# Gates worked out slot by slot, and key and value loads asked for one pair of chunks earlier

## The chip, the cores and the metric

The kernel runs on one core of a Trainium2 chip. The metric is device time in microseconds (us) from start to end of one execution, as a median of several. A profiled execution gives the trace from which every row below comes; its span runs from the first to the last recorded instruction. PE is the matrix engine, DVE the vector engine, ACT the scalar engine, POOL the general engine (it also issues the indirect DMAs, by row numbers in a table), SP the queue that issues the plain DMAs. DMA engines are the sixteen engines that move the data.

## The reference

Two stages. The first is an attention with 32 memory slots for each of 8 heads and 8 batches of 576 tokens; the second a mixture of experts that sends each token to one of 8 experts.

```python
a = softmax(phi, over the 576 tokens)
k_m, v_m = a^T k, a^T v                       # 32 x 64 for each batch and head
attn = softmax(q k_m^T / 8)                   # 576 x 32
x = (attn v_m), heads side by side            # 4608 rows of 512
logits = x @ w_gate                           # 8 for each row
e = argmax(logits)
gate = softmax(logits)[e]
eom = sigmoid((x @ w_output_gate)[e])
out = gate * eom * (relu(x @ w1[e]) @ w2[e])  # 512 -> 1024 -> 512
```

So each row of x needs its 8 gate logits, 8 logits of the output gate, the number of its expert, and one factor, gate * eom, that is multiplied into its output row. All is in fp32; the expert products are made with a high and a low part of each operand.

## The kernel before, in words

**The head: attention.** The batches go in four pairs. Of each pair, `memory` builds the memory keys and values from nine chunks of k and v: `turn_a` transposes the softmaxed phi (tile `ph`) into `at`, `sums` multiplies it with the chunk of k and v (tile `kvt`, or `kv8` for the ninth) into `pk`. `loads` is a generator that asks for k and v, two chunks at each step; `sums` steps it once for each pair of chunks that it uses, so `NLD`, the number of steps taken ahead, is how many pairs of chunks are asked for before their use. `kvt` has 8 buffers. Queries (`qt`, three buffers) are asked for by `load_q` right behind the `scores` that used the buffer. The twenty groups of rows (five to a pair) each go through `scores` (PE), `shift` (DVE transposes and takes the maximum, POOL subtracts), `expo` (ACT), `divide` (DVE sum and reciprocal, POOL multiplies), `back` (DVE transposes) and `values` (PE, then ACT copies to `xo`). The list `ORDER` is walked once for each group and sets the order of these pieces of different groups on each engine.

**Rows in DRAM.** `store` writes the finished rows to `xs`. A row has 576 numbers: four parts of 144, each with 128 numbers of x and 16 partial logits (8 of the gate, 8 of the output gate), since the logits ride along in `values`. The fifth group of a pair holds the last 64 tokens of both its batches and is stored by two transfers of 64 rows (L1058). SP works strictly in order, so a store that waits for its rows holds back every load behind it. `defer` puts a function off by a count of steps of `ORDER`; its counts stand in `LATE`.

**Ranking.** When a pair is done, `rank` sums the partial logits (`lg`), finds each row's expert and its place within the expert (DVE, a few small products on PE), and works out gate * eom. `gates_out` then writes this factor, 16 times side by side, over the first 16 partial logits of each row in `xs`: 64 bytes a row, four transfers for a pair. The one-hot rows `Aw` (POOL) and `table` make the lists of rows by which POOL gathers.

**The body: slots.** A slot is up to three blocks of 128 rows of one expert. Here 14 run: five whole slots of three blocks while attention still goes on, then five of three blocks and four of two whose rows are gathered by quarters of a row (`quart`). For each, POOL gathers `xg`, `turn_x` transposes it into a high and a low part, and `several` makes the two products, eight units of weights `w` per slot. ACT casts each to its high part (L587), DVE subtracts for the low part (L602), both into a ring `whl`. After every twelve products of the first half, and after each unit and block of the second, `hook` takes some steps of the pieces that are left: attention, ranking, gathers, stores put off (`kept`, `singly`). `finish_y` multiplies each output row by its factor and scatters it. The body opens at the 18th group (`START`).

Of the kernel before, what the change touches and what calls it, by code (L numbers as in the profile page):

```python
# [48 lines left out]
NLD = 2  # L49
# [8 lines left out]
LATE = {"lg": 8, "w": 2, "ct": 8, "pe": 3, "dve": 2}  # L58
# [13 lines left out]
def attention_moe(tc, phiT, kv, qT, wgo, wall, out):  # L72
# [3 lines left out]
    with contextlib.ExitStack() as ctx:  # L76
# [615 lines left out]
        def loads():  # L692

            load_phi(0)
            for bp in range(NBP):
                for c in (0, 2, 4, 6):
                    load_kv(bp, c)
                    load_kv(bp, c + 1)
                    if bp == 0 and c == 2:
                        load_kv(0, 8)  # L700
                        load_q(0)
                        load_q(1)
                    if bp == 0 and c == PHI1:
                        load_phi(1)
                    if bp == 0 and c == 6:
                        for n in range(2, NQ):
                            load_q(n)
                    if bp == NBP - 1 and c == 6:
                        stream.fetch()
                    yield  # L710

# [220 lines left out]
        def rank(bp, lg):  # L932

            t0 = bp * 2 * S
            lt = lg[:, :, 0:E]
            lo = lg[:, :, E:2 * E]
# [4 lines left out]
            w2_ = rt.tile(b3, F32, name="w2_")  # L941
            w3_ = rt.tile(b3, F32, name="w3_")
            pm = rt.tile([P, NCH], F32, name="pm")
            zs = rt.tile([P, NCH], F32, name="zs")
            gd = rt.tile([P, NCH], F32, name="gd")
# [4 lines left out]
            gt = rt.tile([P, NCH, XQ - P], F32, name="gt")  # L950
# [6 lines left out]
            G.tensor_tensor(w2_[:], lt, lmb, ALU.subtract)  # L957
# [8 lines left out]
            V.tensor_tensor(w3_[:], oh, lo, ALU.mult)  # L966
            A.activation(w2_[:], w2_[:], AF.Exp)
# [5 lines left out]
            V.tensor_reduce(zs[:], w3_[:], axis=AX.X, op=ALU.add)  # L973
            yield

            def rest():
# [10 lines left out]
                V.tensor_reduce(gd[:], w2_[:], axis=AX.X, op=ALU.add)  # L987
                A.activation(zs[:], zs[:], AF.Exp, scale=-1.0)
# [4 lines left out]
                V.tensor_scalar(gd[:], gd[:], 1e-9, None, ALU.add)  # L993
# [3 lines left out]
                V.tensor_scalar(zs[:], zs[:], 1.0, None, ALU.add)  # L997
# [3 lines left out]
                V.tensor_tensor(gd[:], gd[:], zs[:], ALU.mult)  # L1001
                yield
                V.tensor_copy(row[:], ri[:])  # L1003
                V.reciprocal(gd[:], gd[:])
                yield
                V.tensor_copy(gt[:], gd[:].unsqueeze(2).to_broadcast([P, NCH, XQ - P]))
                def gates_out(b):
                    nc.sync.dma_start(
                        xs[t0 + b * S:t0 + b * S + 512, P:XQ].rearrange("(c p) d -> p c d", p=P),
                        gt[:, 4 * b:4 * b + 4])  # L1010
                    nc.sync.dma_start(xs[t0 + b * S + 512:t0 + b * S + 576, P:XQ], gt[64 * b:64 * b + 64, 8])
# [4 lines left out]
                if bp == 1 and "open" not in env:  # L1016
                    kept.extend(functools.partial(gates_out, b) for b in range(2))
                    singly.extend(functools.partial(one_hot, c) for c in range(NCH))
                else:
                    for b in range(2):  # L1020
                        gates_out(b)
                    for c in range(NCH):
                        one_hot(c)
                        if c % 3 == 2:
                            yield
# [17 lines left out]
        def store(bp, c2, xo, lg):  # L1043
            t0 = bp * 2 * S
            b, n = c2 // 2, 2 if c2 < 4 else 1
            if c2 < 4:
                r, w = t0 + b * S + (c2 % 2) * 256, 256 // len(xo)
                for k, t in enumerate(xo):
                    out_ = functools.partial(
                        nc.sync.dma_start, xs[r + w * k:r + w * k + w].rearrange("(c p) d -> p c d", p=P),  # L1050
                        t.rearrange("p c r d -> p c (r d)"))
                    if 5 * bp + c2 in KEPT:
                        kept.append(out_)
                    else:
                        out_()
            else:
                for b_ in range(2):
                    nc.sync.dma_start(  # L1058
                        xs[t0 + b_ * S + 512:t0 + b_ * S + 576],
                        xo[0][64 * b_:64 * b_ + 64, 0].rearrange("p r d -> p (r d)"))  # L1060
# [37 lines left out]
        def turn_x(z, c):  # L1098
# [4 lines left out]
            if c == 0:  # L1103
                z["x"] = (mo.tile([P, 4, 3 * P], F32R, name="xh"),
                          None if nb == 2 else mo.tile([P, 4, 3 * P], F32R, name="xl"))
                if z["quart"]:
                    z["xt"] = {}
                    z["g"] = env["xt"].tile([P, 3], F32, name="gx")
                    for b in range(4):
                        k = nb - (nb == 2 and b > 1)  # L1110
                        A.copy(z["g"][32 * b:32 * b + 32, 0:k], xg[0:32, 0:k, XQ * b + P])
# [25 lines left out]
            V.tensor_tensor(xl[:, c, 0:n], pt, xh[:, c, 0:n].bitcast(F32), ALU.subtract)  # L1137

# [126 lines left out]
        def finish_y(z, k, py):  # L1265
# [9 lines left out]
            A.activation(y[0:n], py[0:n], AF.Copy, scale=z["g"][0:n, k:k + 1] if z["quart"] else z["xg"][:, k, P:P + 1])  # L1275
# [4 lines left out]
        def several(i, st, nxt, hook):  # L1280


            z = order[i]
            nb, x, h = z["nb"], z["x"], []
            n_ = nb * P
            for u in range(4):
# [36 lines left out]
                hook()  # L1323
            py = [bank([DM], "ps") for _ in range(nb)]
# [26 lines left out]
        def single(i, st, nxt):  # L1351
# [15 lines left out]
            for u in range(4):  # L1367
# [13 lines left out]
                if u < 3:  # L1381
                    st.done(PUMP[1])
            for c in range(5):
                nxt(c)
# [132 lines left out]
```

## Time and profile before

| | |
|---|---|
| median of the runs shown | 546.48 us |
| lowest of them | 546.12 us |
| the profiled execution | 548.27 us |
| its span | 546.5 us |
| PE busy in the span | 508.1 us, 93% |
| DVE, ACT, POOL busy | 65%, 53%, 44% |
| mean granted clock of PE | 0.974 of 2.4 GHz |
| bytes moved by DMA | 123.54 MB, 42,062 packets |
| packets under 512 bytes | 10,320 |

Busy shares are of the whole span. A share says nothing on what a stage waits for; that is read from the timeline of an engine and from the waits.

### The profile page before, as it was taken

To read this page: it belongs to the slowest core of one execution; us is meant where nothing else is said; L and a number is where in the kernel's file an instruction comes from. 1 tells how busy PE (TensorE), PEld (TensorE's weight loads), DVE (VectorE), ACT (ScalarE), POOL (GpSimd) and SP (SyncE) were. 2 spreads that over 40 slices of the span, in tenths; PEclk is the share of its full clock that TensorE was granted. 3 is DMA by queue.
4 is the path that set the end of the run, shared out by engine and by line. 5 is a ranking of instruction groups with operands and counts; after the bars stand their busy time and mean duration, and the time that the engine had idled before them with its cause. 6 is when DMAs were issued, how large, how long until landed. Compare 5 with 4: busy or idle time off the path is not lost. (4 is left out here: it accounts for less than half of the span.)

```text
span 546.5 us, 10564 instructions
## 1 busy us (share of the span) xinstructions
PE 508.1 (93%) x3850; PEld 438.2 (80%) x3850; DVE 353.6 (65%) x783; ACT 288.1 (53%) x536; POOL 239.5 (44%) x254
## 2 busy tenths in 40 slices
PE   3888788799999999999999999999999999999993
PEld 2555465598788898898998989998999799898982
DVE  4376979978965569888455547953875397639310
ACT  3467466754445466363443547853874476458210
POOL 2244386582625045220575554465547253721101
PEclk9969879999999999999999999999999999999998
DMA  8999998998767668745566665865785577743001
GB/s 303 418 391 388 411 347 282 365 359 299 228 191 256 196 192 280 225 147 155 155 163 205 184 228 168 257 194 202 217 257 143 187 249 232 239 135 98 30 20 44
DMA packets 42062, 123.54 MB, mean 226 GB/s; under 512 B 10320, under 2 KB 10384, under 8 KB 41616
## 3 DMA queue, kind: packets, MB, share of 16 engines
q1 hardware_dynamic: 35200, 102.71, 57.2%
q0 software_dynamic: 6800, 20.06, 10.6%
q8 instruction: 32, 0.52, 0.4%
q14 instruction: 30, 0.25, 0.1%
HBM read 102.40 MB, written 20.35 MB: 225 GB/s over the span
## 5 line engine op out<-in xcount | busy, mean ns | idle before, releaser
L1340 PE MATMUL bps<-whl,hh 128*128 128x512 f32 x640 | 192.6, 393 | 0.8 <-issue 0.8
L1303 PE MATMUL bps<-xh,whl 128*128 128x384 f32 x640 | 165.8, 336 | 0.0
L602 DVE TENSOR_TENSOR whl<-w,whl 128x1024 fp32r<-128x1024 f32 x112 | 136.4, 1222 | 9.7 <-ACT whl L587 9.3
L1340 PEld LDWEIGHTS bps<-whl,hh 128*128 128x128 f32 x640 | 119.9, 188 | 25.9 <-issue 1.6
L587 ACT CAST whl<-w 128x1024 fp32r<-128x1024 f32 x112 | 116.6, 1046 | 24.8 <-remote 14.4
L1303 PEld LDWEIGHTS bps<-xh,whl 128*128 128x128 f32 x640 | 115.8, 188 | 1.2 <-issue 0.6
L542 POOL DMA_INDIRECT xg<-xs,idx_ql x84 | 99.6, 1186 | 25.6 <-issue 22.6
L1303 PE MATMUL bps<-xl,whl 128*128 128x384 f32 x320 | 107.1, 335 | 0.0
L1340 PE MATMUL bps<-whl,hl 128*128 128x512 f32 x240 | 93.6, 390 | 0.0
L1308 DVE SCALAR_TENSOR_TENSOR hl<-bps,hh 128x384 fp32r<-128x384 f32 x80 | 43.9, 554 | 66.2 <-ACT hh L1307 51.2
L1307 ACT ACTIVATE hh<-bps 128x384 fp32r<-128x384 f32 x80 | 38.9, 493 | 78.7 <-PE bps L1303 70.5
L1276 POOL DMA_INDIRECT out<-y,idx_ol x23 | 25.8, 1122 | 108.5 <-ACT y L1275 54.4
L1303 PEld LDWEIGHTS bps<-xl,whl 128*128 128x128 f32 x320 | 60.1, 188 | 0.5
L1340 PEld LDWEIGHTS bps<-whl,hl 128*128 128x128 f32 x240 | 45.1, 188 | 8.5
L885 POOL TENSOR_TENSOR ea<-ea,mx 128x512 f32<-128x512 f32 (+1 forms) x20 | 19.3, 963 | 45.8 <-DVE mx L883 38.8
L1298 PE MATMUL bps<-xh,whl 128*128 128x384 f32 x128 | 37.7, 338 | 0.0
L1299 PE MATMUL bps<-xh,whl 128*128 128x256 f32 x128 | 35.7, 279 | 0.0
L1014 POOL TENSOR_SCALAR Aw<-iota_row,row 128x128 bf16<-128x128 bf16 x36 | 29.3, 828 | 8.3 <-DVE row L1003 8.3
L1276 POOL DMA_INDIRECT out<-y,idx_ob x9 | 10.7, 1189 | 49.0 <-ACT y L1275 39.5
L1275 ACT ACTIVATE y<-bps,gx 128x512 f32<-128x512 f32 x19 | 13.1, 688 | 35.6 <-PE bps L1340 29.0
L916 PE MATMUL bpd<-ve_b,aT 64*128 64x144 f32 (+1 forms) x320 | 27.9, 325 | 2.5 <-DVE ea L879 1.4
L879 DVE STREAM_TRANSPOSE ea<-bpd 128x512 f32<-128x512 f32 (+1 forms) x20 | 13.2, 660 | 23.7 <-PE bpd L869 11.8
(277 smaller groups left out, 599.7 us busy)
## 6 DMA issues: line engine op xcount, KB each, us to landing
w<-wall SPq DMA_DIRECT2D x112, 512.0 KB
kvt<-kv SPq DMA_DIRECT2D x32, 512.0 KB
qt<-qT SPq DMA_DIRECT2D x16, 512.0 KB
xs<-xo SPq DMA_DIRECT2D x8, 576.0 KB
ph<-phiT SPq DMA_DIRECT2D x3, 1152.0 KB
kv<-kv SPq DMA_DIRECT2D x4, 512.0 KB
xg<-xs,idx_ql POOLq DMA_INDIRECT x84
ph<-phiT SPq DMA_DIRECT2D x4, 288.0 KB
```

Of the source, the lines that this page charges most:

```text
L542: G.indirect_dma_start(out=z["xg"][:, k, XQ * b:XQ * b + XQ], out_offset=None, in_=xs[0:z["rows"]].rearrange("t (a q) -> (t a) q", a=4), i ...
L587: A.copy(hl[:, 0], w[:])
L602: V.tensor_tensor(hl[:, 1], w[:], hl[:, 0].bitcast(F32), ALU.subtract)
L916: T.matmul(px[to:to + n, r, sl], z["aT"][h, o:o + n], ves[2 * bp + b][h, g], start=True, stop=True)
L1014: G.tensor_scalar(Aw[:, bp * NCH + c], iota_row[:], row[:, c:c + 1], None, ALU.is_equal)
L1276: G.indirect_dma_start(out=out, out_offset=bass.IndirectOffsetOnAxis(ap=z["idx"][1][0:n, z["q0"] + k:z["q0"] + k + 1], axis=0), in_=y[0:n] ...
L1298: T.matmul(pb, w[:, 0, o:o + P], x[0][:, cc], start=(cc == 0), stop=False)
L1299: T.matmul(pb[:, 0:256], w[:, 1, o:o + P], x[0][:, cc, 0:256], start=False, stop=(cc == 3))
L1303: T.matmul(pb, w[:, b, o:o + P], x[a][:, cc, 0:n_], start=(n == 0), stop=(n == 11))
L1307: A.activation(h_[:, j], pb, AF.Relu)
L1308: V.scalar_tensor_tensor(l_[:, j], pb, 0.0, h_[:, j].bitcast(F32), ALU.max, ALU.subtract)
L1340: T.matmul(py[k], a, w[:, b, DM * f:DM * f + DM], start=(u == 4 and f == 0 and n == 0), stop=(u == 7 and f == 1 and n == len(ps) - 1))
```

## The change

Each slot gets its rows' logits with the rows, so `gate` works the factor out there. It takes one step at every `hook` of the first half of the slot, ahead of the step of attention, and what is left is drained ahead of the second half. A whole slot sums the four partial logits in one reduction; a slot by quarters brings them together with three copies on ACT and three additions on DVE, in rows of 32 partitions, and copies the factor out by four copies (which stood in `turn_x` before). `rank` loses the matching work, and `gates_out` with its 16 transfers goes. `NLD` is 3 in place of 2, `loads` gets a step of its own at its end that asks for the first weights, and the store of the tenth group (the fifth of the second pair) is put off by five steps.

```diff
-NLD = 2
+NLD = 3
-LATE = {"lg": 8, "w": 2, "ct": 8, "pe": 3, "dve": 2}
+LATE = {"st": 5, "lg": 8, "w": 2, "ct": 8, "pe": 3, "dve": 2}
...
-                    if bp == NBP - 1 and c == 6:
-                        stream.fetch()
                     yield
+            stream.fetch()
+            yield
...
-            G.tensor_tensor(w2_[:], lt, lmb, ALU.subtract)
...
-            V.tensor_tensor(w3_[:], oh, lo, ALU.mult)
-            A.activation(w2_[:], w2_[:], AF.Exp)
...
-            V.tensor_reduce(zs[:], w3_[:], axis=AX.X, op=ALU.add)
...
-                V.tensor_reduce(gd[:], w2_[:], axis=AX.X, op=ALU.add)
-                A.activation(zs[:], zs[:], AF.Exp, scale=-1.0)
...
-                V.tensor_scalar(gd[:], gd[:], 1e-9, None, ALU.add)
...
-                V.tensor_scalar(zs[:], zs[:], 1.0, None, ALU.add)
...
-                V.tensor_tensor(gd[:], gd[:], zs[:], ALU.mult)
...
-                V.reciprocal(gd[:], gd[:])
...
-                V.tensor_copy(gt[:], gd[:].unsqueeze(2).to_broadcast([P, NCH, XQ - P]))
-                def gates_out(b):
-                    nc.sync.dma_start(
-                        xs[t0 + b * S:t0 + b * S + 512, P:XQ].rearrange("(c p) d -> p c d", p=P),
-                        gt[:, 4 * b:4 * b + 4])
-                    nc.sync.dma_start(xs[t0 + b * S + 512:t0 + b * S + 576, P:XQ], gt[64 * b:64 * b + 64, 8])
...
+                def out_():
+                    for b_ in range(2):
+                        nc.sync.dma_start(
+                            xs[t0 + b_ * S + 512:t0 + b_ * S + 576],
+                            xo[0][64 * b_:64 * b_ + 64, 0].rearrange("p r d -> p (r d)"))
+
+                if bp == 1:
+                    defer("st", out_)
+                else:
+                    out_()
...
+        def gate(z):
+
+            nb, xg, quart = z["nb"], z["xg"], z["quart"]
+            n, m = (32, 6 if nb == 2 else 4 * nb) if quart else (P, nb)
+            z["g"] = rt.tile([P, 3], F32, name="gx", bufs=2)
...
+            if quart:
...
+                for a in range(1, 4):
+                    A.copy(lq[:, a - 1, 0:m], xv[32 * a:32 * a + 32])
+                    yield
+                V.tensor_tensor(ls, xv[0:32], lq[:, 0, 0:m], ALU.add)
+                V.tensor_tensor(lq[:, 1, 0:m], lq[:, 1, 0:m], lq[:, 2, 0:m], ALU.add)
+                yield
+                V.tensor_tensor(ls, ls, lq[:, 1, 0:m], ALU.add)
+            else:
+                V.tensor_reduce(ls, xg[:, 0:nb].rearrange("p k (a q) -> p k q a", a=4)[:, :, P:XQ],
+                                axis=AX.X, op=ALU.add)
+            yield
+            V.tensor_reduce(mx, ls[:, :, 0:E], axis=AX.X, op=ALU.max)
+            V.tensor_tensor(oe[:], iota_s[:, 0:E], slot[:, z["s"]:z["s"] + 1].to_broadcast([P, E]), ALU.is_equal)
+            yield
+            V.tensor_tensor(w2, ls[:, :, 0:E], mx.unsqueeze(2).to_broadcast(b3), ALU.subtract)
+            V.tensor_tensor(w3, ls[:, :, E:2 * E], oe[0:n].unsqueeze(1).to_broadcast(b3), ALU.mult)
+            yield
+            A.activation(w2, w2, AF.Exp)
+            V.tensor_reduce(zs, w3, axis=AX.X, op=ALU.add)
+            yield
+            A.activation(zs, zs, AF.Exp, scale=-1.0)
+            V.tensor_reduce(sm, w2, axis=AX.X, op=ALU.add)
+            yield
+            V.tensor_scalar(sm, sm, 1e-9, None, ALU.add)
+            V.tensor_scalar(zs, zs, 1.0, None, ALU.add)
+            V.tensor_tensor(g, sm, zs, ALU.mult)
...
-            A.activation(y[0:n], py[0:n], AF.Copy, scale=z["g"][0:n, k:k + 1] if z["quart"] else z["xg"][:, k, P:P + 1])
+            A.activation(y[0:n], py[0:n], AF.Copy, scale=z["g"][0:n, k:k + 1])
...
+            gen = gate(z)
+
+            def hook():
+                next(gen, None)
+                hook_()
...
+            last(gen)
```

On DVE, where the first pair is ranked beside the first route (`fi`, `pt`, `ie` and `exc` belong to the route, `rki`, `ri` and `row` to the rank, `gd`, `zs` and `gt` to the gates), this stood:

```order
L991 TENSOR_TENSOR w__953<-ohg,pr 128x72
L993 TENSOR_SCALAR gd<-gd 128x9
L174 TENSOR_TENSOR pt<-fi,upto 128x64
L996 TENSOR_REDUCE rki<-w__953 128x9
L997 TENSOR_SCALAR zs<-zs 128x9
L176 TENSOR_REDUCE inc<-pt 128x8
L999 TENSOR_SCALAR ri<-rki 128x9
L1000 TENSOR_SCALAR jg<-rki 128x9
L1001 TENSOR_TENSOR gd<-gd,zs 128x9
L304 TENSOR_SCALAR ie<-inc 128x8
```

Now this stands there:

```order
L978 TENSOR_TENSOR w__957<-ohg,pr 128x72
L174 TENSOR_TENSOR pt<-fi,upto 128x64
L982 TENSOR_REDUCE rki<-w__957 128x9
L176 TENSOR_REDUCE inc<-pt 128x8
L984 TENSOR_SCALAR ri<-rki 128x9
L985 TENSOR_SCALAR jg<-rki 128x9
L304 TENSOR_SCALAR ie<-inc 128x8
```

The steps on `gd` and `zs` are gone from between the others, and nothing else changes its place.

On SP, while the second pair is worked on, this stood from the last writes of the first pair's gates (`gt`) to the last loads of k and v (`kvt`, `kv`); the two transfers of 64 rows of `xo` are the tenth group's:

```order
L1008 DMA xs<-gt 128x4x16
L1011 DMA xs<-gt 64x16
L689 DMA kvt<-kv 128x1024 x2
L684 DMA qt<-qT 128x1024
L689 DMA kv_1268<-kv 128x1024
L689 DMA kvt<-kv 128x1024 x2
L684 DMA qt<-qT 128x512
L684 DMA qt<-qT 128x1024
L1058 DMA xs<-xo 64x576 x2
L689 DMA kvt<-kv 128x1024 x2
L684 DMA qt<-qT 128x1024
L689 DMA kvt<-kv 128x1024 x2
```

Now this stands there:

```order
L689 DMA kvt<-kv 128x1024 x2
L684 DMA qt<-qT 128x1024
L689 DMA kv_1252<-kv 128x1024
L689 DMA kvt<-kv 128x1024 x2
L684 DMA qt<-qT 128x512
L684 DMA qt<-qT 128x1024
L689 DMA kvt<-kv 128x1024 x2
L684 DMA qt<-qT 128x1024
L1033 DMA xs<-xo 64x576 x2
```

The writes of `gt` are gone, the tenth group's store stands behind the last loads of k and v, and each pair of chunks is asked for one step sooner.

On DVE, in the first slot (`hl` and `whl` belong to the slot, `sa` and `aT` to attention), this stood:

```order
L1308 SCALAR_TENSOR_TENSOR hl<-bps,hh 128x384
L602 TENSOR_TENSOR whl<-w,whl 128x1024 x2
L895 TENSOR_REDUCE sa<-ea_207 128x16
L897 RECIPROCAL sa<-sa 128x16
L903 STREAM_TRANSPOSE aT<-ea_206 128x512
L1308 SCALAR_TENSOR_TENSOR hl<-bps,hh 128x384 x2
L602 TENSOR_TENSOR whl<-w,whl 128x1024
L1308 SCALAR_TENSOR_TENSOR hl<-bps,hh 128x384
```

Now this stands there (`gl`, `gs`, `oe`, `gw` and `go` are the gates' tiles):

```order
L1340 SCALAR_TENSOR_TENSOR hl<-bps,hh 128x384
L602 TENSOR_TENSOR whl<-w,whl 128x1024 x2
L1141 TENSOR_REDUCE gs<-gl 128x3
L1142 TENSOR_TENSOR oe<-iota_s,slot 128x8
L895 TENSOR_REDUCE sa<-ea_207 128x16
L897 RECIPROCAL sa<-sa 128x16
L903 STREAM_TRANSPOSE aT<-ea_206 128x512
L1340 SCALAR_TENSOR_TENSOR hl<-bps,hh 128x384
L1144 TENSOR_TENSOR gw<-gl,gs 128x24
L1145 TENSOR_TENSOR go<-gl,oe 128x24
L1340 SCALAR_TENSOR_TENSOR hl<-bps,hh 128x384
L602 TENSOR_TENSOR whl<-w,whl 128x1024
```

The gates' steps stand between those of the slot and of attention, one or two at each hook.

## Rows read from the trace of the kernel before

**Rows 1.** The page's first part: busy us (share of the span) xinstructions.

```profile
PE 508.1 (93%) x3850; PEld 438.2 (80%) x3850; DVE 353.6 (65%) x783; ACT 288.1 (53%) x536; POOL 239.5 (44%) x254
```

**Rows 2.** Timeline of PE: start, length, what, and in brackets the wait before.

```profile
62.03 0.64 PE L778 MATMUL pk<-kvt,at 128*32 128x128 f32 x16 [1.36 <-DMA kvt<-kv]
...
72.72 0.94 PE L869 MATMUL bpd<-qt,kT 64*32 64x256 f32 x16 [1.00 <-ACT kT L809]
...
75.92 2.46 PE L916 MATMUL bpd<-ve_b,aT 64*128 64x144 f32 x16
...
80.50 0.92 PE L869 MATMUL bpd<-qt,kT 64*32 64x256 f32 x16
...
111.72 0.47 PE L1303 MATMUL bps<-xh,whl 128*128 128x384 f32 x1
```

**Rows 3.** Windows: stretch, PE, PEld, DVE, ACT, POOL busy, PE clock, DMA share, GB/s.

```profile
57.00:78.50 21.50, 16.65 (x287) 11.57 (x283) 19.58 (x78) 10.19 (x25) 12.03 (x19) 0.82 1.01 377
78.50:82.40 3.90, 3.90 (x59) 2.26 (x53) 0.71 (x4) 2.47 (x6) 3.24 (x4) 0.67 0.99 381
82.40:112.00 29.60, 24.56 (x459) 16.97 (x458) 26.88 (x68) 20.56 (x43) 19.89 (x24) 0.94 0.91 320
...
111.70:125.00 13.30, 13.30 (x101) 12.17 (x100) 10.66 (x19) 6.32 (x11) 10.99 (x11) 1.00 1.01 379
125.00:150.00 25.00, 24.71 (x181) 20.41 (x181) 21.32 (x61) 12.27 (x22) 10.55 (x14) 1.00 0.81 250
```

**Rows 4.** Waits of PE from 112 us on: sum in us, times, longest.

```profile
PE bpd L916 <- DVE xl L1137: 1.1, 1, 1.1
```

**Rows 5.** Timeline of DVE in the head.

```profile
59.65 0.23 DVE L966 TENSOR_TENSOR w__955<-ohg,lg 128x72 f32<-128x72 bf16 x1
...
65.32 0.23 DVE L991 TENSOR_TENSOR w__953<-ohg,pr 128x72 f32<-128x72 bf16 x1 [0.40 <-PE pr L985]
...
66.69 0.30 DVE L1006 COPY gt<-gd 128x144 f32<-128x144 f32 x1
...
74.67 0.18 DVE L244 CAST hl_i<-pr 128x12 bf16<-128x12 f32 x1 [0.59 <-PE pr L237]
...
82.39 0.72 DVE L879 STREAM_TRANSPOSE ea<-bpd 128x512 f32<-128x512 f32 x1 [3.19 <-PE bpa L804]
...
89.41 1.33 DVE L956 TENSOR_TENSOR w__1478<-lg,lm 128x72 f32<-128x72 f32 x1
...
95.08 0.33 DVE L966 TENSOR_TENSOR w__1480<-ohg,lg 128x72 f32<-128x72 bf16 x1
...
98.60 0.62 DVE L997 TENSOR_SCALAR zs<-zs 128x9 f32<-128x9 f32 x1
...
99.72 0.30 DVE L1006 COPY gt<-gd 128x144 f32<-128x144 f32 x1
```

**Rows 6.** Windows of 3 us in the head, columns as in rows 3.

```profile
72.00:75.00 3.00, 1.89 (x34) 1.16 (x38) 2.27 (x9) 1.29 (x5) 3.00 (x7) 0.88 1.02 292
75.00:78.00 3.00, 3.00 (x46) 2.46 (x36) 2.90 (x9) 1.06 (x2) 1.21 (x2) 0.50 0.89 296
...
84.00:87.00 3.00, 2.38 (x46) 1.33 (x39) 2.87 (x9) 2.42 (x6) 2.81 (x4) 1.00 0.69 228
```

**Rows 7.** DVE, one line at a time: shortest, median, longest ns, first and last start.

```profile
L1066 DVE TENSOR_REDUCE lg<-xo x12: 214/361/371, 40.6 to 180.6; 128x32 f32<-128x128 f32 x8, 128x16 f32<-128x64 f32 x4
...
L1001 DVE TENSOR_TENSOR gd<-gd,zs x4: 156/162/166, 66.1 to 211.1; 128x9 f32<-128x9 f32 x4
```

**Rows 8.** Waits of PE from 57 to 112 us, the same columns as rows 4.

```profile
PE pk L778 <- DMA kvt<-kv: 1.9, 2, 1.4
```

**Rows 9.** Timeline of SP round the tenth group's store.

```profile
82.39 2.81 SPq L684 DMA_DIRECT2D qt<-qT  x2
88.44 1.59 SPq L1058 DMA_DIRECT2D xs<-xo  x2
```

**Rows 10.** Timeline of POOL.

```profile
89.55 1.04 POOL L898 TENSOR_TENSOR ea<-ea,sa 128x512 f32<-128x512 f32 x1
```

More of the change, by code (lines that the diff above doesn't have):

```diff
@@ L932, in rank @@
         def rank(bp, lg):
-            t0 = bp * 2 * S
             lt = lg[:, :, 0:E]
-            lo = lg[:, :, E:2 * E]
             b3 = [P, NCH, E]
@@ L940, in rank @@
             w1_ = rt.tile(b3, F32, name="w1_")
-            w2_ = rt.tile(b3, F32, name="w2_")
-            w3_ = rt.tile(b3, F32, name="w3_")
             pm = rt.tile([P, NCH], F32, name="pm")
-            zs = rt.tile([P, NCH], F32, name="zs")
-            gd = rt.tile([P, NCH], F32, name="gd")
             oc = rt.tile([P, E], F32, name="oc")
@@ L949, in rank @@
             row = rt.tile([P, NCH], F32, name="row", bufs=2)
-            gt = rt.tile([P, NCH, XQ - P], F32, name="gt")
             oh = ohg[:, cs]
@@ L1016, in rest @@
                 if bp == 1 and "open" not in env:
-                    kept.extend(functools.partial(gates_out, b) for b in range(2))
                     singly.extend(functools.partial(one_hot, c) for c in range(NCH))
                 else:
-                    for b in range(2):
-                        gates_out(b)
                     for c in range(NCH):
@@ L1056, in store @@
             else:
[L1057 to L1060, printed above, removed]
+                def out_():
[7 more added lines that the diff above has]
+                    out_()
             n = n // len(xo)
@@ L1107, in turn_x @@
                     z["xt"] = {}
[L1108 to L1111, printed above, removed]
             xh, xl = z["x"]
@@ L1137, in turn_x @@
             V.tensor_tensor(xl[:, c, 0:n], pt, xh[:, c, 0:n].bitcast(F32), ALU.subtract)
+        def gate(z):
+            nb, xg, quart = z["nb"], z["xg"], z["quart"]
+            n, m = (32, 6 if nb == 2 else 4 * nb) if quart else (P, nb)
+            z["g"] = rt.tile([P, 3], F32, name="gx", bufs=2)
+            tl, mm = (env["xt"], 12) if quart else (rt, 3)
+            ls, w2, w3 = (tl.tile([n, mm, w], F32, name=nm, bufs=1)[:, 0:m]
+                          for nm, w in (("gl", 2 * E), ("gw", E), ("go", E)))
+            sm_ = tl.tile([n, 4, mm], F32, name="gs", bufs=1)
+            mx, sm, zs, g = (sm_[:, i, 0:m] for i in range(4))
+            oe = rt.tile([P, E], F32, name="oe")
+            b3 = [n, m, E]
+            if quart:
+                xv = xg[:, 0:nb].rearrange("p k (b q) -> p (k b) q", b=4)[:, 0:m, P:XQ]
+                lq = env["hs"].tile([P, F], F32, name="hs")[0:32, 0:576].rearrange("p (a j l) -> p a j l", a=3, l=2 * E)
+                for a in range(1, 4):
[24 more added lines that the diff above has]
+            V.tensor_tensor(g, sm, zs, ALU.mult)
+            if not quart:
+                V.reciprocal(z["g"][:, 0:nb], g)
+                return
+            V.reciprocal(g, g)
+            yield
+            for b in range(4):
+                k = nb - (nb == 2 and b > 1)
+                A.copy(z["g"][32 * b:32 * b + 32, 0:k], g[:, b:4 * k - 3 + b:4])
@@ L1278, in finish_y, with several @@
                 in_=y[0:n], in_offset=None, bounds_check=NTOK - 1, oob_is_err=False)
-        def several(i, st, nxt, hook):
+        def several(i, st, nxt, hook_):
             z = order[i]
+            gen = gate(z)
+            def hook():
+                next(gen, None)
+                hook_()
             nb, x, h = z["nb"], z["x"], []
@@ L1382, in single @@
                     st.done(PUMP[1])
+            last(gate(z))
             for c in range(5):
```

## The prediction

> **What bounds the kernel now.** I began with the page's busy times [rows 1]: PE is busy for 508.1 us of 546.5, so 38 us at most are to be had on it. The windows say where. From 111.7 us on, where the first product of the body starts [rows 2], PE is busy in 13.30 of 13.30 us and then in 24.71 of 25.00 [rows 3], and the longest of its waits on another engine from there to the end adds up to 1.1 us [rows 4]. The body is bound by PE alone: its length does not depend on what DVE, ACT, POOL or the DMAs do, as long as PE finds its operands ready. So the time of the kernel is the moment at which the body opens, plus a fixed rest; what is saved before 111.7 us comes off the end whole, and what is saved behind it comes off nowhere.
>
> Then I read what paces the head. From 57.0 to 78.5 us DVE is busy for 19.58 of 21.50 us, and from 82.4 to 112 us for 26.88 of 29.60, while PE has 4.9 and 5.0 us free [rows 3]. Between them lie 3.9 us in which DVE does 0.71 us of work: it stands for 3.19 us ahead of a transposition [rows 5], since the scores that it reads start at 80.50 us only [rows 2]. In that stretch PE is busy throughout at a granted clock of 0.67, a mix of its two levels, 2.4 and 1.2 GHz; from 75 to 78 us it was 0.50, that is 1.2 GHz, after a window in which PE had worked for 1.89 of 3.00 us [rows 6]. The DMA engines are at a share of 1.01 from 57.0 to 78.5 us and 0.91 later [rows 3]. So DVE sets the pace for most of the later head, PE for some 4 us, and the DMAs are close behind.
>
> **The gates leave the ranking.** Each pair's rank loses eight DVE instructions. For the first pair they run from the first L966 at 59.65 us to L1006 at 66.69, for the second from 95.08 to 99.72 [rows 5]. Their recorded lengths overlap the next one's, so I take from each start to the next start: 1.0 us for the eight of the first pair, 1.8 us for the eight of the second, where L997 alone took 0.62 us in place of about 0.16 [rows 5, 7]. Both lie in the stretches that DVE fills, so both come off the opening: 2.8 us, term A. It is between 0, if another engine is late by as much at the same place, and 2.8. The ranks of the third and fourth pair lie behind 111.7 us and are worth nothing. The subtraction on POOL and two short exponentials on ACT go from each rank as well; these engines have some 9 us or more free in each of the long stretches [rows 3], and I count nothing for them; should POOL be late, their absence only helps.
>
> **The gates' transfers go.** Sixteen transfers of 64 bytes a row leave SP, four of them in the head, issued at about 70 us. Their mark is the window from 72 us: a DMA share of 1.02, but 292 GB/s, where the stretch around it has 377 [rows 3, 6], so about 0.7 us of the DMA engines' time per 3 us. Between 57 and 112 us PE waited for k and v twice [rows 8], both times ahead of these transfers, so I count 0; at most it is those 0.7 us and as much in the next window, 1.4 us.
>
> **k and v a pair earlier.** At 62.03 us PE waited 1.36 us for a chunk of k and v [rows 2], and for the next chunk the rest of 1.9 us [rows 8]. Asked for one pair of chunks sooner, that is by 4 to 10 us, these land in time. But DVE paces there. What the late PE cost DVE is 0.40 us at 65.32 and 0.59 us at 74.67 [rows 5], both times waiting for small products that stand behind these on PE. So I count 1.0 us, term B, between 0 and 1.9. What becomes late instead: the queries behind the loads that moved ahead. A pair of chunks is 1.05 MB, at 377 GB/s [rows 3] 2.8 us; queries are asked for three groups ahead, some 15 us, so they can bear it.
>
> **The tenth group's store.** SP is through with its queries at 85.20 us, then stands until 88.44 before it issues the store [rows 9], with the loads of k and v behind it. The DMA share falls to 0.69 meanwhile [rows 6]. Behind the loads, the store stops nobody for long: queued after it are the first weights, asked for as `loads` ends, and the rows' gather is far off. PE does not wait for k or v behind the stall [rows 8], so I count 0, and at most the 0.9 us of idle DMA time in that window.
>
> **The gates in the slots.** A whole slot adds a reduction of 128x192, near the 0.361 us of the 128x128 one [rows 7], so 0.5 us, and ten small instructions at 0.16 to 0.23 us [rows 5, 7]: 2.4 us on DVE. A slot by quarters has thirteen, at most 3 us, plus three copies and two exponentials on ACT. Over 14 slots that is near 39 us of DVE, which is idle for 193 of the span's 546.5 us [rows 1]. Behind each waiting gate step on DVE stand the low parts `hl` and `whl`, for which PE waits in the end; it finds them ready today [rows 4]. From 111.7 to 150 us DVE has 6.3 us free [rows 3]; two gates need 4.8 and the third pair's rank gives back 1.0 to 1.8. It fits, so I count 0, term C; its other end is the third rival.
>
> One thing could make those instructions dearer. L956 took 1.33 us, a form that takes 0.23 elsewhere [rows 5]; it ended at 90.74 us, just behind a POOL operation that ran from 89.55 to 90.59 [rows 10]. The Trainium skill, in "SBUF — State Buffer", section "Who interferes with whom", says that a DVE operation with both inputs in SBUF contends with GpSimd's reads, and whichever issues second stands still until the first is done. The trace agrees on the length, though the record shows DVE starting 0.14 us first. By that rule the four or more such instructions of each gate would cost the third rival's price; by rows 9, the small price above.
>
> **The sum.** A 2.8 and B 1.0: 3.8 us earlier. The profiled execution took 548.27 us with a span of 546.5; 1.77 us lie around the span and stay, so it would become 544.5. It was 1.8 us above the median of the runs, 546.48, to which the forecast refers: 546.48 - 3.8 = **542.7 us**. A difference below 2%, 10.9 us, is about what a measurement of this kernel cannot tell from no change.
>
> **Rivals.** First: the gap of 3.19 us on DVE closes too. For it: PE's clock fell after a window with 1.1 us of idling, 1.00 us of it on ACT's copy of `kT` [rows 2, 6], and with k and v there in time PE comes to that place sooner; at 2.4 GHz the products at 75.92 us would take about half of their 2.46 us, and with the other work to 80.5 the scores would be about 3 us sooner. Against: the copy stands behind exponentials that wait for DVE, and they stay. It gives 542.7 - 3.2 = 539.5.
>
> Second: DVE's instructions are not what holds the head, but the ring DVE, POOL, ACT, PE through which each group passes, or the DMAs with their share of 1.01. Then A is swallowed and only part of B shows: 0.5 us, 546.0. For it: four engines are over half busy from 82.4 us on [rows 3]. Against: DVE is idle for 2.7 us there.
>
> Third, the one that ends slower: in the first two slots the gates' instructions meet POOL's subtractions and products of attention and stand as L956 did, 1.1 us more for each of six in a gate. Two gates take 4.8 + 13 us where DVE has 6.3 free and up to 1.8 given back, so the low parts are 9 to 10 us late and PE with them: 542.7 + 9.5 = 552. It decides from 0.24 us extra per instruction on (6.3 + 1.4 - 4.8 = 2.9 us, over twelve). Against: L1001 never took over 0.166 us in four places [rows 7], and low parts have several units' time to spare.
>
> Fourth: asking earlier does not bring k and v sooner, since the DMAs are full, and pushes a query past its use by the 2.8 us of one pair, with A still saved in part: 548.
>
> **How the numbers follow.** Forecast 0.45, own range 541 to 545 (A whole or half, B between its ends); gap closes too 0.22; swallowed 0.18; slots late 0.10; query late 0.05. The range takes in the first and the second rival with their bounds (the first with the 1.4 and 0.9 us of DMA time down to 537) and the fourth up to 548.5, and leaves out the third and the tails. Faster by over 2% needs less than 535.6: the first rival with all the bounds together, 0.04. Slower needs more than 557.4, the third at more than its price, 0.04. Within 2%: 0.92.
>
> **What would show it.** The first product of the body (now 111.72) near 108 us; no wait on k or v at the second pair's second two chunks; DVE as full as now but shorter by 2.8 us; the granted clock from 73 to 81 us telling the forecast from the first rival; PE in the body with waits of some 1 us. The prediction is wrong if PE's waits in the first two slots grow by several us, or if the opening does not move.

## The result, and the profile after

The changed kernel takes 553.26 us (median of 6 runs), the kernel before 546.58 in the same comparison: ratio 1.0127, 95% interval 1.0094 to 1.016, that is 5 to 9 us slower, where 3.8 us faster was forecast. The profiled execution took 556.98 us, the longest of the six; its span is 555.3 us. Single executions far slower than the rest, such as one of the kernel before at 997 us and one of `e7_pad_four` below at 1717 us, stay out of the ratios and intervals.

The page's first part, after, answers to [rows 1]:

```profile
PE 511.8 (92%) x3850; PEld 439.4 (79%) x3850; DVE 376.5 (68%) x923; ACT 300.6 (54%) x583; POOL 244.3 (44%) x250
```

DVE has 23 us more work, PE the same products. The first product of the body, after, answers to the last of [rows 2]; behind it the waits of PE from there to the end, which answer to [rows 4]:

```profile
113.98 0.44 PE L1335 MATMUL bps<-xh,whl 128*128 128x384 f32 x1
```

```profile
PE bps L1335 <- DVE xl L1113: 4.0, 8, 0.7
PE pr L237 <- DVE bwl L229: 1.7, 1, 1.7
PE bpd L916 <- DVE xl L1113: 1.1, 1, 1.1
```

The third row is old; the other two are new. The body, from that product to PE's last end, takes 432.45 us (113.98 to 546.43), before 425.67 (111.72 to 537.39): 6.8 us more, as much as the whole loss of the medians, 6.7.

To place it, I measured each half of each slot by the starts of its products. Two things stand out. The first halves of the four three-block slots that follow a two-block slot take 18.25 to 18.33 us in place of 16.67: 6.4 us. (The first row of waits names 4.0 of them; the ends of products are modelled, and a late product's record is longer, 0.44 us in place of 0.34, so I go by the starts.) The second half of the fourth of the five whole slots takes 21.44 in place of 19.67: 1.8 us; the expectations below call it the third. (Before, one second half had been 1.25 us longer than its likes.) Windows of one two-block slot and of the three-block slot behind it, before and then after (columns as in [rows 3]):

```profile
381.54:399.99 18.45, 18.45 (x105) 16.89 (x104) 16.14 (x31) 14.29 (x29) 10.05 (x8) 1.00 0.75 226
```

```profile
386.98:405.43 18.45, 18.45 (x106) 16.89 (x104) 15.37 (x40) 13.01 (x30) 11.08 (x8) 1.00 0.67 202
405.43:440.04 34.61, 33.62 (x169) 30.04 (x168) 23.23 (x45) 20.98 (x38) 18.61 (x16) 1.00 0.70 209
```

The two-block slot itself is no longer than it was, 18.45 us; the bill comes in the next. DVE was busy there for 16.14 of 18.45 us even before (after, 15.37: part of its work has slid into the next slot). In the last 6 us of the two-block slot DVE makes `xt` and `xl` for the next one. Its timeline before, from the last `hh` of the first half on:

```profile
393.52 0.62 DVE L1318 SCALAR_TENSOR_TENSOR hh<-hl,hh 128x128 fp32r<-128x128 f32 x2
394.06 1.03 DVE L1118 STREAM_TRANSPOSE xt<-xg 128x384 f32<-128x384 f32 x2
...
400.02 0.55 DVE L1137 TENSOR_TENSOR xl<-xt,xh 128x384 fp32r<-128x384 f32 x1
```

and after:

```profile
400.36 0.61 DVE L1350 SCALAR_TENSOR_TENSOR hh<-hl,hh 128x128 fp32r<-128x128 f32 x2
400.90 0.18 DVE L1148 TENSOR_REDUCE gs<-go 32x6 f32<-32x48 f32 x1
401.01 0.18 DVE L1151 TENSOR_REDUCE gs<-gw 32x6 f32<-32x48 f32 x1
401.23 0.16 DVE L1153 TENSOR_SCALAR gs<-gs 32x6 f32<-32x6 f32 x1
401.36 0.16 DVE L1154 TENSOR_SCALAR gs<-gs 32x6 f32<-32x6 f32 x1
401.55 0.15 DVE L1155 TENSOR_TENSOR gs<-gs 32x6 f32<-32x6 f32 x1
401.74 0.18 DVE L1159 RECIPROCAL gs<-gs 32x6 f32<-32x6 f32 x1
402.11 1.04 DVE L1094 STREAM_TRANSPOSE xt<-xg 128x384 f32<-128x384 f32 x2 [0.19 <-DMA xg<-xs,idx_ql]
...
408.06 0.55 DVE L1113 TENSOR_TENSOR xl<-xt,xh 128x384 fp32r<-128x384 f32 x1
```

Before, the last `xl` ends at 400.57, 0.58 us after the slot that reads it begins (399.99). After, it ends at 408.61, 3.18 us behind that slot's start (405.43), and PE stands:

```profile
407.06 0.44 PE L1335 MATMUL bps<-xl,whl 128*128 128x384 f32 x1 [0.24 <-DVE xl L1113]
...
408.66 0.45 PE L1335 MATMUL bps<-xl,whl 128*128 128x384 f32 x1 [0.74 <-DVE xl L1113]
```

Of the six gate rows (`gs`) the last five are the drain; the first is the step of the first half's last hook, and seven more instructions of the gate stand ahead of it. By the start of that last `hh` DVE is already 1.4 us later in the slot than before (13.38 us into it, before 11.98); the six rows add the other 1.2.

### The profile page after: what moved, and what is told of

Its sections match the earlier page's. It is cut to its first block, busy times and chain, and to the rows that moved or that the text cites. A ratio compares the mean times of both kernels' runs of the same rounds, so it can differ in the third digit from the quotient of the medians.

```text
span 555.3 us, 10699 instructions
## 1 busy us (share of the span) xinstructions
PE 511.8 (92%) x3850; PEld 439.4 (79%) x3850; DVE 376.5 (68%) x923; ACT 300.6 (54%) x583; POOL 244.3 (44%) x250
## 5 line engine op out<-in xcount | busy, mean ns | idle before, releaser
L542 POOL DMA_INDIRECT xg<-xs,idx_ql x84 | 108.1, 1287 | 25.6 <-issue 24.4
L1302 POOL DMA_INDIRECT out<-y,idx_ol x23 | 24.1, 1048 | 109.0 <-ACT y L1301 59.7
L1301 ACT ACTIVATE y<-bps,gx 128x512 f32<-128x512 f32 x34 | 23.4, 688 | 66.5 <-PE bps L1373 34.8
```

The lines of the kernel that those rows point to most:

```text
L542: G.indirect_dma_start(out=z["xg"][:, k, XQ * b:XQ * b + XQ], out_offset=None, in_=xs[0:z["rows"]].rearrange("t (a q) -> (t a) q", a=4), i ...
L1302: G.indirect_dma_start(out=out, out_offset=bass.IndirectOffsetOnAxis(ap=z["idx"][1][0:n, z["q0"] + k:z["q0"] + k + 1], axis=0), in_=y[0:n] ...
```

## The experiments

Ratios are to the kernel before on the same chip, with 95% intervals.

**One part alone.** `e1_two_pairs` is the changed kernel with `NLD = 2` and the first weights asked for as before; `e2_three_pairs_alone` is the kernel before with the other loads.

```diff
-NLD = 2
+NLD = 3
-                    if bp == NBP - 1 and c == 6:
-                        stream.fetch()
                     yield
+            stream.fetch()
+            yield
```

> The changed kernel with k and v asked for two pairs of chunks ahead, as before; all else stays. Theory 1 (asking three pairs ahead pushes the query of the fifth group behind k and v: PE waits about 2 us for it near 39 us and then runs at 1.2 GHz): the wait goes, the body opens near 108 us in place of 114, the body keeps its loss of some 7 us, so 549 to 550 us. Rival (the depth of the loads is not at fault, the head is late for another reason): like the changed kernel, 553.

> The kernel before with k and v asked for three pairs ahead and nothing else of the change. Theory 1: the same wait for the fifth group's query and the low clock behind it, without the gates' relief on the vector engine, so the body opens 4 to 6 us later: 550 to 552 us. Rival: the earlier loads take away the 1.9 us of waits for k and v and cost nothing: 545 to 546.6.

Measured: `e1_two_pairs` 554.17 us, 1.0133 (1.0087 to 1.018), body 432.36. `e2_three_pairs_alone` 544.39 us, 0.9939 (0.9922 to 0.9956), body 424.74. Both theories fail. The loads are not guilty; alone they gain 3.3 us (2.4 to 4.3), more than the rival's 1.9. Beside the gates that gain cannot be seen: `e1_two_pairs` and the changed kernel lie within each other's intervals. The loss belongs to the rest of the change.

**More of the gate earlier.** In slots by quarters every hook takes two steps, so that nothing is left for the drain, in the changed kernel (`e3_gate_two_steps`) and with `NLD = 2` (`e4_both`).

```diff
                 next(gen, None)
+                if z["quart"]:
+                    next(gen, None)
                 hook_()
```

> The changed kernel, but in slots by quarters the gate takes two steps at each hook, so that nothing of it is left to drain at the middle of the slot. Theory 2 (the drain stands ahead of the transposes by which the next slot's rows are made ready, and in slots of two blocks these had only 1 us to spare): PE's waits on the low part xl go from 4 us to near 0, the four slots of three blocks that follow a slot of two are 1.6 us shorter each, so 553.3 - 6.4 = 547. Rival (the gates' work is too much for the vector engine wherever it stands): 552 to 554.

> Both edits: two pairs ahead and two gate steps at a hook. Theories 1 and 2 together: the head 3 to 4 us shorter than before, the body 1.7 us longer (the wait for the row lists that stays): 544 to 545.5 us, faster than both kernels. If only theory 1 holds 549 to 550, if only theory 2 holds 547.

Measured: 558.67 us, 1.021 (1.0137 to 1.0283), and 558.27, 1.0211 (1.0169 to 1.0252). Worse. The waits of PE in `e3_gate_two_steps`, and ACT's timeline in the first half of one of its two-block slots:

```profile
PE bps L1337 <- DVE xl L1113: 6.2, 12, 0.8
```

```profile
338.48 0.53 ACT L1349 ACTIVATE hh<-hl 128x384 fp32r<-128x384 f32 x1 [0.98 <-DVE hl L1345]
...
342.20 0.53 ACT L1349 ACTIVATE hh<-hl 128x384 fp32r<-128x384 f32 x1 [1.19 <-DVE hl L1345]
```

In the changed kernel the waits at this place are 0.42 to 0.79 us. The early steps stand ahead of `hl`, for which ACT waits, and DVE then for ACT. My hope that only the drain's place mattered fell here.

**The drain behind the transpositions.** `e5_drain_behind`:

```diff
-            last(gen)
             py = [bank([DM], "ps") for _ in range(nb)]
...
                 if u == 7:
+                    last(gen)
                     finish_y(z, k, py[k])
```

> The changed kernel, but what is left of a slot's gate at the middle of the slot is not drained there: the steps go on at the hooks of the second half and are drained just ahead of the first finish_y. Theory (the drain stands ahead of the transpositions of the next slot on a full DVE, so the low parts xl come late, 1.6 us at each of the four slots that follow a two-block one): the four first halves fall from 18.25 to about 16.7 us and the time from 553.3 to near 547. Rival (DVE and ACT have too much to do in a two-block slot, wherever the steps stand): the waits for xl stay and the time stays within 551 to 555. Second rival (the gate now comes late for finish_y, and the next slot with it): the halves stay long, with y waiting for gx, 553 to 558.

Measured: 548.59 us, 1.0025 (1.0003 to 1.0047); the four halves take 17.7 to 17.8 us. A part of the theory: 1.6 us became 1.05, since the gate's other steps stay in the two-block slot, and those of the drain now stand between the transpositions.

**No gates in the slots.** `e6_no_gates`:

```diff
-            gen = gate(z)
-            def hook():
-                next(gen, None)
-                hook_()
+            z["g"] = env["one"]
+            hook = hook_
```

> The changed kernel without its gates: each output row is multiplied by one in place of gate * eom, and nothing is computed in its place; ranking has lost its gates too, so the head is that of the changed kernel. Theory (the cost is in the slots, 6.8 us of the body): the body takes 425 to 426 us again, as in the kernel before, and the time is 544 to 546; what lies between it and the three-pairs-alone kernel (544.4) is then what the gates' absence from the head is worth, near 0. Rival (term A of the prediction is real, but hidden by the body's loss): 541 to 542.5. Second rival (the loss comes from elsewhere, the tenth group's store or another order of the lists): 550 or more.

Measured: 544.69 us, 0.9949 (0.9924 to 0.9974); body 424.25, the four halves 16.67, the fourth whole slot's second half 19.65. All 8.2 us between this body and the changed kernel's (four times 1.6, and 1.8) are the gates.

**The same time on DVE without a gate.** In the kernel before, two-block slots alone; `e8_pad_one` has a 1 in place of the 4:

```diff
+            if nb == 2:
+                for o, c, m in 4 * ((192, P, 64), (256, 0, P)):
+                    V.scalar_tensor_tensor(h_[:, :, o:o + m], sh[:, :, c:c + m], 0.0,
+                                           h_[:, :, c:c + m].bitcast(F32), ALU.max, ALU.subtract)
             py = [bank([DM], "ps") for _ in range(nb)]
```

> The kernel before; in each of the four two-block slots the last pair of DVE instructions of the first half (the low part hh of the fourth unit) is made five times in place of once, with the same result. That is 8 more instructions of 0.33 us, 2.6 us of DVE, at the place where the drain stands in the changed kernel, and nothing else. Theory (the margin of the low part xl in front of the next slot is about 1 us): PE waits for xl at each of the four following slots, 1.0 to 1.7 us each, and the time is 4 to 7 us more than the kernel before, near 552. Rival (it is the back and forth of ACT and DVE in the gate, not DVE's time, that delays): no wait, 546 to 548.

> As the run with four, but the pair is made once more only: 0.66 us of DVE in each two-block slot. Theory (margin of about 1 us): nothing to be seen, 546 to 547.5, within 0.2% of the kernel before. Rival (no margin at all, each us on DVE there is a us on PE): 4 x 0.66 = 2.6 us more, 549.

Measured: 551.94 us, 1.0066 (1.0033 to 1.0099), and 547.87, 1.0014 (0.9998 to 1.0029). DVE in `e7_pad_four`, then PE:

```profile
396.35 2.25 DVE L1326 SCALAR_TENSOR_TENSOR hh<-hl,hh 128x128 fp32r<-128x128 f32 x8
398.52 1.02 DVE L1118 STREAM_TRANSPOSE xt<-xg 128x384 f32<-128x384 f32 x2
...
404.40 0.55 DVE L1137 TENSOR_TENSOR xl<-xt,xh 128x384 fp32r<-128x384 f32 x1
```

```profile
405.01 0.44 PE L1303 MATMUL bps<-xl,whl 128*128 128x384 f32 x1 [0.75 <-DVE xl L1137]
```

The padding took 2.17 us, a little less than I had put; the halves grew by 1.05 us each. No gate, no ACT in it: DVE's time at that place is enough. One pair is free, as a margin near 1 us asks.

**The gate a slot ahead.** `e10_gate_a_slot_ahead`: a two-block slot's gate is stepped in the second half of the three-block slot ahead of it.

```diff
-            gen = gate(z)
+            gen = iter(()) if z.get("gated") else gate(z)
...
                     nxt(TURN[nb].index(step))
+                    if nb == 3 and z["quart"] and step == TURN[3][0] and i + 1 < st.hi // 8 and order[i + 1]["nb"] == 2:
+                        gen, order[i + 1]["gated"] = gate(order[i + 1]), True
...
+            last(gen)
```

> The changed kernel, but the gate of a two-block slot is worked out in the second half of the three-block slot ahead of it, a step at each hook from the second block on, where PE works for 16.4 us and DVE has idle time; nothing is left of it in the two-block slot. Theory (the place alone is what costs, not the amount of work): the first halves behind the two-block slots go from 18.25 to 16.7 us, the body is 425 to 427.5 us (1.7 us at a whole slot may stay), and the time is 545 to 547.5, ratio 0.995 to 1.0. Rival (the amount of work costs, DVE and ACT being late by it wherever it stands): 550 or more, with the loss at other halves.

Measured: 545.01 us, 0.9966 (0.994 to 0.9992), body 426.19. Its windows for the same two slots, to be held against those of the changed kernel above:

```profile
380.03:398.48 18.45, 18.45 (x105) 16.89 (x104) 15.86 (x35) 13.53 (x28) 9.66 (x8) 1.00 0.72 212
398.48:431.51 33.03, 33.03 (x170) 30.19 (x168) 22.54 (x50) 20.45 (x41) 19.02 (x15) 1.00 0.73 213
```

The same work, and PE busy for 33.03 of 33.03 us. At these four slots the place alone cost; the 1.8 us at the fourth whole slot stay (21.03 us).

These traces give the margin. For the slots behind a two-block slot (typical of four), from the rows of `xl` and of PE:

| kernel | last `xl` ends after the slot's start, us | first half, us |
|---|---|---|
| before | 0.58 | 16.67 |
| `e8_pad_one` | 1.04 | 16.67 |
| `e10_gate_a_slot_ahead` | 1.40 | 16.67 |
| `e5_drain_behind` | 2.62 | 17.71 |
| `e7_pad_four` | 2.64 | 17.72 |
| changed kernel | 3.18 | 18.26 |
| `e3_gate_two_steps` | 3.97 | 19.07 |

Up to 1.40 nothing is lost; from 2.62 on the half is longer by the end less 1.6 us (2.62 - 1.05, 2.64 - 1.05, 3.18 - 1.59, 3.97 - 2.40). One half lies between: in `e13_whole_late_again`, below, an `xl` that ends 1.69 us after the start gives 16.79 us, 0.13 more, and 1.69 - 0.13 is 1.56. For `e3_gate_two_steps` the table has one of the two halves at a granted clock of 1.00; the other two, both at 0.92, took 20.5 to 20.6 us. So the kernel before had 1.6 - 0.58, about 1.0 us, to spare at each of these slots, and no row of its waits shows that.

**The head.** `e9_loads_and_store` is the kernel before with the loads and the tenth group's store of the changed one; `e11_rank_relieved` is `e6_no_gates` with `NLD = 2` and the store as before, so that only the ranking's relief is left.

```diff
-NLD = 2
+NLD = 3
...
-LATE = {"lg": 8, "w": 2, "ct": 8, "pe": 3, "dve": 2}
+LATE = {"st": 5, "lg": 8, "w": 2, "ct": 8, "pe": 3, "dve": 2}
...
+                if bp == 1:
+                    defer("st", out_)
+                else:
+                    out_()
```

> The kernel before with NLD 3, the step of its own for the first weights, and the tenth group's store put off by five steps: the changed kernel's head without any change to the gates. Theory (the loads give the gain of the three-pairs-alone kernel, 0.6%, and the store nothing): ratio to the kernel before 0.992 to 0.996, 543 to 545.5. Rival (the store saves the 0.9 us that the prediction gave as its bound): 1 us below that, ratio near 0.992 or less. Second rival (the store late makes the gather late): 546 or more.

> The kernel before with all work on the gates left out: no gate in the ranking, no transfers of gates, none in the slots; each output row is multiplied by one. NLD is 2 and the tenth group's store stands where it was. What is left is term A of the prediction by itself, with the absence of the 16 transfers. Term A whole (2.8 us): 544.5 to 545.5, ratio 0.994 to 0.996. Swallowed (second rival of the prediction): ratio 0.998 to 1.001, 547 to 548.

Measured: 544.66 us, 0.9946 (0.9928 to 0.9965), and 547.5, 0.999 (0.9969 to 1.0011). No gain of the store shows beside the loads (0.9946 with it, 0.9939 without; the intervals are too wide to exclude 0.9 us), and term A is 0.5 us (-0.6 to 1.7). The waits of PE from 57 to 112 us in `e11_rank_relieved`, answering to [rows 8], and its window from 57 us, to [rows 3]:

```profile
PE bpd L869 <- DMA qt<-qT: 4.2, 2, 3.6
PE pk L778 <- DMA kvt<-kv: 2.8, 3, 2.1
```

```profile
57.00:78.50 21.50, 16.45 (x292) 10.90 (x292) 17.60 (x64) 10.51 (x23) 11.51 (x18) 0.84 1.01 393
```

DVE has 2 us less to do in that stretch, the DMA engines are as full as before, and PE waits for loads: 3.5 us in that window. DVE's wait for the small product, 0.40 us at 65.32 before [rows 5], is 2.03 us here.

**The whole slots.** `e12_whole_late` is `e10_gate_a_slot_ahead` with the gate of a whole slot begun at the sixth block of its second half.

```diff
+            half = [z["quart"]]
             def hook():
-                next(gen, None)
+                if half[0]:
+                    next(gen, None)
                 hook_()
...
+                half[0] |= step >= 5
                 if u == 7:
+                    if not z["quart"]:
+                        last(gen)
                     finish_y(z, k, py[k])
```

> As the run with the two-block slot's gate a slot ahead, and the gate of a whole slot begins only in the second half of its slot, at the sixth block of twelve, behind the stretch of the third whole slot in which DVE makes the lists bwl. Theory (PE's 1.7 us wait for bwl there is the same thing as the waits for xl: gate steps ahead of a chain that has no time to spare): the second half of the third whole slot goes from 21.0 to about 19.7 us, the body from 426.2 to 424.5 to 425.0, and the time to 543 to 545, about the three-pairs-alone kernel. Rival (lists late for another reason, such as the head's order): 21 us again, 545 to 546.5.

Measured: 558.57 us, 1.011 (1.0045 to 1.0176), where the kernel before took 552.7. The fourth whole slot's second half took 19.61 us as expected, but stalls that the profile puts down to nothing stood elsewhere (waits of PE from 105 us on):

```profile
PE bps L1377 <- issue: 4.8, 6, 1.4
```

So it was run once more, on another chip, beside `e10_gate_a_slot_ahead`.

> The kernel of the run before this one once more, beside the one with only the two-block slots' gates moved: in that run the third whole slot's second half took 19.61 us, as expected, but stalls put down to issue, of all engines, stood in the fourth and fifth whole slots, and the kernel before was slower and uneven there too (547 to 555 us). If the stalls belong to that chip: the body is 424.5 to 425.5 us and the time 543 to 545. If they belong to the kernel (gates late in whole slots hold ACT and with it the casts): first or second halves of the fourth and fifth whole slots are long again by several us, 552 or more, while the kernel beside it stays at 545.

> The kernel with the gate of a two-block slot worked out a slot ahead, for the comparison on one chip: 0.9966 of the kernel before, as measured, with the second half of the third whole slot at 21.0 us. If the other kernel's theory holds, this one is 1.0 to 1.6 us slower than it.

Measured: 544.78 us, 0.996 (0.9932 to 0.9988), body 425.67, and 544.36, 0.9928 (0.9902 to 0.9954). The long halves are gone; they did not come from the kernel. DVE's last list rows and PE's wait for them in the changed kernel's fourth whole slot, which starts at 229.75 us:

```profile
254.10 1.06 DVE L229 TENSOR_TENSOR bwl<-eq,tok_hl 128x405 bf16<-128x405 bf16 x2
```

```profile
255.22 0.53 PE L237 MATMUL pr<-bwl,Aw 128*128 128x90 bf16 x9 [1.65 <-DVE bwl L229]
```

and in `e13_whole_late_again`, where that slot starts at 230.19, with its second half's window:

```profile
252.70 1.06 DVE L229 TENSOR_TENSOR bwl<-eq,tok_hl 128x405 bf16<-128x405 bf16 x2
```

```profile
247.12:266.74 19.62, 19.62 (x126) 16.12 (x125) 16.20 (x40) 7.79 (x13) 0.97 (x1) 1.00 0.48 142
```

The lists end 25.4 us into the slot with the gate ahead of them, 23.6 without; before, 23.7. It is the same thing as with `xl`: with the gate there this half took 20.7 us or more in every trace, without it 20.2 or less. The 1.8 us did not show in the time: other halves had become longer by up to 0.85 us, and the two kernels cannot be told apart. That misses what both expectations asked for, 1.0 to 1.6 us between them.

## Why the prediction was wrong

**The step that failed is term C**, with the sentence under it: "PE finds its operands ready", so the body's length does not depend on DVE. Its amount was about right: put at 3 us of DVE at most for a gate by quarters, it is 2.4 us in a two-block slot and up to 3.3 in a three-block one, by records that overlap. Its cover was read from sums: free time over the span and over the stretch from 111.7 to 150 us. That stretch was taken for two slots; it is not quite the first one (111.72 to 154.94), and in the first two nothing is lost. The prediction named `hl` and `whl` as the parts behind the gates' steps, not `xl`, and gave low parts "several units' time to spare" without measuring one. The slots that decide are the two-block ones, which I had not looked at: 2.3 us of DVE free in 18.45, and a last `xl` with 1.0 us to spare. A gate there delays it by 2.6 us (3.18 - 0.58); 1.6 us are left over, four times. A list of waits shows where the margin is already negative, never how thin it is elsewhere.

**Term A** was 2.8 us and measured 0.5 (-0.6 to 1.7); the second rival had it right that it is swallowed, though not that the loads give little. That DVE was busy for 91% of a stretch did not make it the pace: the DMA share there was 1.01. What held the relieved head, the trace of `e11_rank_relieved` suggests (loads) but no run isolates.

**Term B** was 1.0 us with a bound of 1.9; the loads alone give 3.3 (2.4 to 4.3). The waits for k and v do go: they stand in no row of PE's waits of the changed kernel behind 27 us. I priced them by what DVE had visibly lost from PE being late, 0.99 us. The waits themselves, from 27 to 112 us in the trace of before, were nearer:

```profile
PE pk L778 <- DMA kvt<-kv: 2.8, 4, 1.4
```

**The opening and the first rival.** The first product of the body was to come near 108 us and came at 113.98. One profile cannot settle this: with the same head it came between 107.22 (`e5_drain_behind`) and 113.33 us (`e13_whole_late_again`); with the head of before at 111.72, 112.12 (`e7_pad_four`) and 109.68 (`e8_pad_one`). So A and B are judged by the medians. Nor was the gap of 3.19 us, which the first rival would close, a property of the kernel: in `e7_pad_four` and `e8_pad_one`, whose heads are those of before, it is 0.53 us. In `e8_pad_one`:

```profile
79.29 0.72 DVE L879 STREAM_TRANSPOSE ea<-bpd 128x512 f32<-128x512 f32 x1 [0.53 <-PE bpd L869]
```

The granted clock from 73 to 81 us was 1.00 in that execution, 0.58 in the one from which the prediction was read:

```profile
73.00:81.00 8.00, 7.60 (x122) 5.22 (x120) 5.41 (x17) 3.72 (x9) 5.90 (x8) 0.58 0.94 314
```

```profile
73.00:81.00 8.00, 6.75 (x136) 4.59 (x138) 7.20 (x23) 5.00 (x15) 5.64 (x8) 1.00 0.99 351
```

**The zeros.** The store shows no gain, as put. The fourth rival (a query pushed past its use): PE waited 2.0 us for a query at 40.90 us in the changed kernel, but the three-pairs kernel gains all the same with such a wait of 1.8, and waits of 3.3 to 3.6 us stand in `e7_pad_four`, `e8_pad_one` and `e11_rank_relieved`, with `NLD = 2`; no loss by it shows.

**The third rival** was the one on the right side, 552 us, and for the wrong reason: it had gates in the first two slots standing as L956 did. From 127.28 to 152.28 us PE is busy for 24.71 of 25.00 us, as before. L1145, both of whose inputs lie in SBUF, takes 0.241 us at the most in all 14 slots. Of all the gates' steps with two inputs one alone stood, in the first slot, for 0.13 us more than the 0.175 of its likes, and it ends just behind a product of POOL:

```profile
124.64 0.30 DVE L1144 TENSOR_TENSOR gw<-gl,gs 128x24 f32<-128x24 f32 x1
```

```profile
123.86 1.05 POOL L898 TENSOR_TENSOR ea<-ea,sa 128x512 f32<-128x512 f32 x1 [0.24 <-DVE sa L897]
```

So the rule of the Trainium skill's "SBUF — State Buffer", "Who interferes with whom", which the rival had beside it, shows in the gates once at most, and the price of 1.1 us in none of them. L1154, with one tile as its input, took 0.41 us in place of 0.16 in four three-block slots, each time until within 0.04 us of the end of an indirect DMA on POOL; why is not isolated, and the halves in which it falls are no longer than before. (The small price that the prediction takes from "rows 9" stands in [rows 7]. The form of L956 does take 0.235 us elsewhere, at 124.9 and 181.1 us; the rows of 0.23 in [rows 5] are of other lines.)

Against what the body lost, 8.2 us by `e6_no_gates`, that kernel is 2.8 us (1.4 to 4.2) faster than before: 5.4 slower together, where 6.7 (5 to 9) were measured. The sum of the forecast for the head, 3.8, was in reach, by wrong shares; the body's 0 was not. The prediction took differences below 2% for too small to tell; this one of 1.3% is clear of its interval.

## What to carry to other kernels

An engine without waits still has margins: for each operand that is made while another is used, hold the end of its last part against the moment at which it is needed, in the shortest stage, before work is put ahead of it; here what went beyond the margin cost PE its full length. Free time is to be summed within the stage that pays, and added work put where its engine has it: here one stage earlier, which made the loss at the four slots vanish (545.0 us). Leaving the gates where they were and asking for k and v earlier takes 544.4 us, and no version with gates in the slots beats that beyond doubt. One more thing for reading: a gap or a fall of the clock in one profile may belong to that execution; another run with the same code up to there shows it.

## What the runs showed that was not expected

The loss followed the lateness of one operand to within 0.03 us in four kernels that delay it in different ways. On DVE six values on 32 partitions (L1155, 0.15 us) take about as long as nine on 128 (L1001, median 0.162 [rows 7]): for such steps the number of instructions counts, not their size. The Trainium skill, "Perfetto Trace Analysis", "Identifying the Most-Contended Engine", takes the engine with the highest occupancy for the one to work on, and judges TensorE by its weight loads rather than its products. Here PE is the fullest in every two-block slot either way (products 18.45 of 18.45 us, weight loads 16.89, DVE 16.14), and still up to 2.1% of the time hung on when DVE does its work there. On one chip several engines stalled with no cause in the profile; only a second chip told that from the edit.
